# Expert 0 in one tile per batch, its first-batch tile computed between attention and experts

## The chip, the cores and the metric

The kernel runs on one core of a Trainium2 chip. A core has TensorE for matrix products, VectorE and ScalarE for elementwise work, GpSimd for odd jobs and for transfers by a list of addresses, and SyncE, which issues most transfers. Each engine works through its own instruction list in order and waits on semaphores for the others. The metric is the device time of one execution in microseconds (us).

## The reference

Three layers follow each other, for 2 batches of 768 tokens and a width of 512. First an attention in 8 heads of 64, where a query sees only the keys of its own cluster. Then a mixture of 8 experts:

```python
for b in range(B):
    prev_e = -1
    for s in range(S):
        fresh_e = int(np.argmax(logits[b, s]))
        if s == 0 or local_gate[b, s] < 0.5: e = fresh_e
        else: e = prev_e if prev_e >= 0 else fresh_e
        prev_e = e
        ...
        h = np.maximum(x[b, s] @ w1[e], 0.0)
        out[b, s] = p[e] * (h @ w2[e])
```

So each token goes to one expert, and which one depends on the tokens before it in its batch. `w1[e]` is 512 x 1024 and `w2[e]` 1024 x 512. Last comes a gated convolution over the tokens with two 512 x 512 products.

## The kernel before

**Precision.** Products of the experts are made in a fast format (fp32r) from split operands: a value is a high part (cast on ScalarE) plus a low part (the remainder, subtracted on VectorE). A product is three matmuls: high x high, low x high, high x low.

**Attention** runs over 96 items (a head, 128 queries) in 16 groups of 6, in one loop over `i`. Each item has scores (`do_S`), a row maximum on VectorE, an exponential on ScalarE, six transposes and their copies (`do_T`); products with the values follow one group later. Small pieces of other work are put at fixed values of `i`. The first batch is items 0 to 47 and its tokens are routed at items 54 to 69; the third quarter of the tokens is routed within the last group, the last quarter after it.

**Routing a quarter** (`route_steps`, r1 to r5) turns 384 tokens' logits into slot numbers: three small transposes on TensorE (r2p), a scan along the tokens on VectorE (r3), transposes back (r3p), a one-hot and counting matmuls (r4, r4p), slot numbers (r5). Then GpSimd scatters the 384 rows in three transfers (line 612) to `xslots` in DRAM, a list of slots per expert. Experts in `HALVED` have a list for each batch. A row has its 512 values, its gate value and its token number.

**Between attention and experts.** When the last routing matmuls are issued, TensorE computes on constants (`keep_warm` and the loops at lines 851 to 858) until the rows of expert 0 have been scattered and read back (`load_x(0)`, line 1002).

**Experts** are taken in 8 places `k`; four have a fixed expert (`AT`), the four others are ordered by their counts, which SyncE reads as registers (`turn`, line 1124). `CAPS[k]` is the number of slots that a place computes; what exceeds it goes through an overflow loop, which did not run in this execution. For each place `load_x` fetches rows, `do_x` transposes them (four transposes per tile of 128) and splits them, `do_mm1` makes the first layer (2 halves x 4 blocks x 3 terms x 4 depths = 96 matmuls over all columns, into hidden units high and low), and `do_mm2` the second (per tile of 128 rows, 24 matmuls of 512 columns), scaled and scattered by token number to `x2d`.

**Weights** of a place are four pieces of 1 MB, two of the first layer and two of the second. `worder` is the order in which pieces are used and `j` the index in it. `w_dma(j)` loads a piece into one of three staging buffers, `w_split(j, half)` splits half a piece: one ScalarE cast (line 342), one VectorE subtraction (line 343). Split pieces live in a ring of four. A list `work` holds splits and loads to come, and `tick()` takes one of them after each quarter of a first layer and each half tile of a second, besides steps of `overflow_steps` and of the conversion of the final weights.

**Memory.** Pools are stacked. When attention's SBUF pools close, staging buffers, ring and experts' tiles take their place, and their first writers wait for the last users of what lies below.

## Time and profile before

| what | us |
|---|---|
| median of 3 runs (lowest, highest) | 554.32 (554.28, 554.47) |
| the profiled execution's own time | 553.66 |
| span of its trace, first to last instruction | 551.6 |
| TensorE busy, VectorE busy, ScalarE busy | 530.4, 390.3, 333.9 |
| 108.22 MB moved, mean 196 GB/s | |

Times of the trace count from the first instruction. The time of an execution has 2.1 us around its span; the profiled one is 0.66 us under the median. A busy TensorE is not a useful one: constant matmuls count as busy, and matmuls overlap, so the pitch is read from the distance of starts and not from the length of one.

### The profile page before, as it was taken

What the parts mean: (1) busy time and instruction counts of PE and PEld (TensorE: products, weight loads), DVE (VectorE), ACT (ScalarE), POOL (GpSimd) and SP (SyncE); (2) the same over time, 40 slices, a digit from 0 to 9 for tenths busy, and PEclk for the clock granted to TensorE, in tenths of its full rate; (3) what the DMA queues carried; (4) which work ended last, traced back from release to release, by engine and by line L of the source; (5) the groups of instructions that cost most, each with busy time, mean ns of one, the idle gap of its engine ahead of it and who ended that gap; (6) DMA issues with size and microseconds to landing.
All of it is one profiled execution on the core that took longest, in us unless ns stands there. A gap on an engine that the chain in (4) does not pass through costs nothing. (4 is left out here: it accounts for less than half of the span.)

```text
span 551.6 us, 9244 instructions
## 1 busy us (share of the span) xinstructions
PE 530.4 (96%) x3393; PEld 425.4 (77%) x3394; DVE 390.3 (71%) x686; ACT 333.9 (61%) x612; POOL 108.0 (20%) x109
## 2 busy tenths in 40 slices
PE   7898999999999999998789999999999989999996
PEld 3766767776777767767589898878989788899885
DVE  5685767675787776636557988949896893499960
ACT  3696778676777777764145555637465564385642
POOL 4111010020212040111200234162435324100000
PEclk9899999999999999999899999999999999999999
DMA  5776797888784857221658767676876777640023
GB/s 144 218 165 201 166 302 170 265 211 252 215 252 144 212 164 159 106 76 55 219 213 297 229 231 272 213 289 220 293 276 243 243 241 262 211 192 0 20 95 114
DMA packets 35672, 108.22 MB, mean 196 GB/s; under 512 B 5096, under 2 KB 5608, under 8 KB 31016
## 3 DMA queue, kind: packets, MB, share of 16 engines
q1 hardware_dynamic: 31751, 98.61, 58.0%
q0 software_dynamic: 2912, 8.41, 4.0%
q10 hardware_dynamic: 960, 0.58, 0.4%
q8 instruction: 27, 0.44, 0.3%
q14 instruction: 22, 0.17, 0.1%
HBM read 58.83 MB, written 29.39 MB: 160 GB/s over the span
## 5 line engine op out<-in xcount | busy, mean ns | idle before, releaser
L652 DVE TENSOR_REDUCE mx<-s 128x1 f32<-128x768 f32 x96 | 91.5, 954 | 59.4 <-PE s L645 53.1
L681 ACT COPY pt<-tp 128x384 f32<-128x384 f32 x148 | 65.8, 484 | 53.7 <-PE tp L676 53.7
L661 ACT ACTIVATE pexp<-s,mx 128x768 f32<-128x768 f32 x96 | 87.2, 909 | 6.1 <-DVE mx L652 5.0
L343 DVE TENSOR_TENSOR wlo<-wraw,whi 128x1024 fp32r<-128x1024 f32 x62 | 86.9, 1417 | 4.9 <-ACT whi L342 4.6
L676 PE MATMUL tp<-ident,pexp 128*128 128x128 f32 x576 | 81.2, 277 | 0.3 <-DVE pt L679 0.2
L676 PEld LDWEIGHTS tp<-ident,pexp 128*128 128x128 f32 x576 | 68.2, 142 | 7.6 <-ACT pt L681 3.4
L342 ACT CAST whi<-wraw 128x1024 fp32r<-128x1024 f32 x64 | 65.0, 1047 | 8.5 <-DMA wraw<-in_wq_dram 8.5
L688 PE MATMUL pv<-pt,vt 128*64 128x384 f32 x360 | 67.8, 498 | 0.2 <-ACT ut L697 0.2
L641 PE MATMUL s<-st 128*128 128x384 f32 x188 | 57.4, 386 | 1.6 <-ACT pexp L661 1.5
L1082 PE MATMUL yp<-whi,hhi 128*128 128x512 f32 (+4 forms) x136 | 53.7, 395 | 0.8 <-PEq L1147 0.8
L1083 PE MATMUL yp<-wlo,hhi 128*128 128x512 f32 (+4 forms) x136 | 53.7, 395 | 0.1
L1084 PE MATMUL yp<-whi,hlo 128*128 128x512 f32 (+4 forms) x136 | 53.5, 393 | 0.0
L645 PE MATMUL s<-st 80*128 80x384 f32 x188 | 48.9, 341 | 1.3 <-DMA st<-ohr 1.3
L1061 ACT ACTIVATE hhi<-hps 128x512 fp32r<-128x512 f32 (+4 forms) x36 | 19.4, 538 | 45.2 <-PE hps L1057 42.9
L641 PEld LDWEIGHTS s<-st 128*128 128x128 f32 x188 | 28.6, 191 | 18.5 <-ACT pt L681 7.4
L1057 PE MATMUL hps<-xhi,whi 128*128 128x256 f32 (+4 forms) x256 | 41.6, 284 | 0.7 <-ACT xhi L1031 0.7
L1057 PE MATMUL hps<-xhi,wlo 128*128 128x256 f32 (+4 forms) x256 | 41.0, 281 | 0.7 <-DVE wlo L343 0.7
L1057 PE MATMUL hps<-xlo,whi 128*128 128x256 f32 (+4 forms) x256 | 41.1, 281 | 0.1
L688 PEld LDWEIGHTS pv<-pt,vt 128*64 128x64 f32 x360 | 21.9, 136 | 24.1 <-issue 23.7
L1062 DVE SCALAR_TENSOR_TENSOR hlo<-hps,hhi 128x512 fp32r<-128x512 f32 (+4 forms) x36 | 21.6, 608 | 23.4 <-ACT hhi L1061 20.8
L361 POOL TENSOR_TENSOR xx<-xkq,xx 128x768 fp32r<-128x768 f32 x8 | 14.5, 1817 | 117.8 <-ACT xx L355 117.8
L1057 PEld LDWEIGHTS hps<-xhi,whi 128*128 128x128 f32 x256 | 35.2, 189 | 1.7 <-ACT xhi L1031 1.1
(263 smaller groups left out, 928.9 us busy)
## 6 DMA issues: line engine op xcount, KB each, us to landing
wraw<-in_wq_dram SPq DMA_DIRECT2D x30, 1024.0 KB, 6.1
st<-xx SPq DMA_DIRECT2D x48, 384.0 KB, 4.0
xslots<-padrow SPq DMA_DIRECT2D x14, 771.0 KB, 11.9
xkq<-in_kq_dram SPq DMA_DIRECT2D x15, 384.0 KB, 4.3
wspace<-in_wd_dram SPq DMA_DIRECT2D x8, 512.0 KB
xall<-xnat SPq DMA_DIRECT2D x4, 771.0 KB
vt<-in_v_dram SPq DMA_DIRECT2D x8, 384.0 KB, 3.3
out_dram<-os SPq DMA_DIRECT2D x11, 256.0 KB, 2.0
```

The costliest lines, as they stand in the source:

```text
L342: nc.scalar.copy(hi[:, c], t[:, c])
L343: (lo_eng or nc.vector).tensor_tensor(lo[:, c], t[:, c], hi[:, c].bitcast(F32), op=ALU.subtract)
L641: nc.tensor.matmul(ps[:, n, :384], st[:, 1, q0:q0 + 128], st[:, 0, 384 * n:384 * n + 384], start=True, stop=False)
L652: nc.vector.tensor_reduce(mx, ps[:, :, :384], axis=AX.XY, op=ALU.max, negate=True)
L661: nc.scalar.activation(pt, ps[:, :, :384], AF.Exp, bias=mx[:, 0:1], accum_out=Zt[i // 6][:, t, h:h + 1])
L676: nc.tensor.transpose(tp[:, k, :], p[:, 128 * kt:128 * kt + 128], ident)
L681: nc.scalar.copy(dst, tp)
L688: nc.tensor.matmul(PVs[u][64 * h:64 * h + 64, :], Vt[g][:, kt, h, :], PT[u, h][:, kt, :], start=(kt == 0), stop=(kt == NQT - 1), skip_grou ...
L1057: nc.tensor.matmul(hp, a[:, d, fs], c[:, d, :w], start=(n + d == 0), stop=(n + d == 5))
L1082: nc.tensor.matmul(yp[:r], hhi[:, fa, ts], whv[:, f, :], start=(q == 0 and f == 0), stop=False)
L1083: nc.tensor.matmul(yp[:r], hhi[:, fa, ts], wlv[:, f, :], start=False, stop=False)
L1084: nc.tensor.matmul(yp[:r], hlo[:, fa, ts], whv[:, f, :], start=False, stop=(q == 1 and f == 3))
```

## The change

Expert 0 becomes an expert with a list for each batch (`HALVED`), and its place computes 128 slots, those of the second batch. The rows of its first-batch list are loaded at item 84 of attention (`early_load`), and transposed and split at item 89 (`early_rows`). The matmuls on constants go; in their place stand the 96 first-layer matmuls of this tile (`early_products`), put between the routing steps of the last quarter as 17, 11, 5 and the rest, into two PSUM banks `eh`. All four weight pieces of expert 0 now come first in `worder`. Pieces 2 and 3 are loaded by SyncE before the last quarter is routed, 4 and 5 behind the splits of 1 and 2, all ahead of `load_x(0)`; pieces 3 and 4 were loaded by GpSimd before, after expert 1's rows had come. VectorE subtracts pieces 1, 2 and 3 and makes the early tile's low parts behind the slot numbers, and the copies for `turn` come after these. The second layer of the early tile opens the experts' part, with `do_x(0)` before its last two blocks. Then come first and second layer of the second-batch tile, and expert 1. The constants of attention move to a pool that closes with it, and two input pools move to the right end of SBUF, where they stay until the early products are done.

```diff
...
-CAPS = (256, 256, 300, 240, 224, 184, 256, 256)
+CAPS = (128, 256, 300, 240, 224, 184, 256, 256)
...
-HALVED = (1, 2)
+HALVED = (0, 1, 2)
...
-    xin_p = apool("xin", 1)
-    xx_p = apool("xx", 1)
+    early_pools = ExitStack()
+    epool = lambda name: early_pools.enter_context(tc.tile_pool(name=name, bufs=1, side="right"))
+    xin_p = epool("xin")
+    xx_p = epool("xx")
+    acst = apool("acst")
...
-    cd = cst.tile([128, 4, 32], F32, name="cd")
-    cent_sb = cst.tile([128, 4, 64], F32, name="cent_sb")
+    cd = acst.tile([128, 4, 32], F32, name="cd")
+    cent_sb = acst.tile([128, 4, 64], F32, name="cent_sb")
...
-    worder = []
-    for k in range(E):
-        worder += [(k, 0), (k, 1)]
-        if k:
-            worder += [(k - 1, 2), (k - 1, 3)]
+    worder = [(0, 0), (0, 1), (0, 2), (0, 3), (1, 0), (1, 1)]
+    for k in range(2, E):
+        worder += [(k, 0), (k, 1), (k - 1, 2), (k - 1, 3)]
...
     def w_split(j, half, lo_eng=None):
         if worder[j][0] == E:
             return
+        w_high(j, half)
+        w_low(j, half, lo_eng)
+
+    def w_high(j, half):
         rp = ring(j)
...
+        nc.scalar.copy(hi[:, c], wraw[j][:, c])
+
+    def w_low(j, half, lo_eng=None):
+        hi, lo = W[worder[j]]
+        c = slice(1024 * half, 1024 * half + 1024)
         t = wraw[j]
-        nc.scalar.copy(hi[:, c], t[:, c])
         (lo_eng or nc.vector).tensor_tensor(lo[:, c], t[:, c], hi[:, c].bitcast(F32), op=ALU.subtract)
 
 
...
+    EA = {}
+
+    def early_load():
+        EA["xs"] = xin_p.tile([128, 2, S], F32, tag="x", name="exs")[:, 0, :XC]
+        nc.sync.dma_start(EA["xs"], xslots[0:128, :])
+
+    def early_rows():
+        xs = EA["xs"]
+        ids = EA["ids"] = small.tile([128, 1], I32, tag="eids", name="eids", bufs=1)
+        nc.vector.tensor_copy(ids, xs[:, 513:514])
+        pw = EA["pw"] = small.tile([128, 1], F32, tag="epw", name="epw", bufs=1)
+        nc.vector.tensor_copy(pw, xs[:, 512:513])
+        xp = ps_m.tile([128, 512], F32, tag="m", name="exp")
+        for d in range(4):
+            nc.tensor.transpose(xp[:, 128 * d:128 * d + 128], xs[:, 128 * d:128 * d + 128], ident)
+        xx = xx_p.tile([128, 4, S], F32R, tag="xx", name="exx")
+        hi, lo = EA["x"] = xx[:, 0, :512], xx[:, 1, :512]
+        nc.scalar.copy(hi, xp)
+        nc.vector.tensor_tensor(lo, xp, hi.bitcast(F32), op=ALU.subtract)
 
...
+        if i == 84:
+            early_load()
+        if i == 89:
+            early_rows()
     while route:
         route.pop(0)()
     last_PV(2)
+    eh = ps_s.tile([128, 2, 512], F32, tag="s", name="eh")
+    nc.vector.memset(eh[:, 1, :], 0.0)
...
+    w_dma(3)
     moe = ExitStack()
     mpool = lambda name, bufs=1, **k: moe.enter_context(tc.tile_pool(name=name, bufs=bufs, **k))
     ring1 = mpool("ring1", R - 1)
     rings[1] = ring1
-    for n, f in enumerate(route_steps(3)):
-        if n == 1:
-            last_rows()
-        f()
-
-    keep_warm(ps_t.tile([128, 512], F32, tag="t", name="spin3"), 10)
-    spin4 = ps_t.tile([128, 512], F32, tag="t", name="spin4")
-    for w in (128, 192, 224, 256):
-        for _ in range(8):
-            nc.tensor.matmul(spin4[:, :w], onesr[:, :128], onesr[:, :w], start=True, stop=True)
-    for w in (128, 192, 288):
-        for _ in range(6):
-            nc.tensor.matmul(spin4[:, :w], onesr[:, :128], onesr[:, w:2 * w] if w < 256 else onesr[:, :w], start=True, stop=True)
-
+    h_p = mpool("hp", 1)
+    WX = (max(CAPS[0::2]), max(CAPS[1::2]))
+    ehhi, ehlo = [h_p.tile([128, 8, WX[1]], F32R, tag=f"h{t}1", name=f"eh{t}") for t in ("hi", "lo")]
+
+    def early_products():
+        xhi, xlo = [t.rearrange("p (d c) -> p d c", d=4) for t in EA["x"]]
+        for q in range(2):
+            whv, wlv = [t.rearrange("p (d f) -> p d f", d=4) for t in W[0, q]]
+            terms = ((whv, xhi), (whv, xlo)), ((wlv, xhi),)
+            for part in (terms if q else (terms[0] + terms[1],)):
+                for f in range(4):
+                    for a, c in part:
+                        for d in range(4):
+                            yield nc.tensor.matmul(
+                                eh[:, q, 128 * f:128 * f + 128], a[:, d, 128 * f:128 * f + 128], c[:, d, :],
+                                start=(q == 0 and a is whv and c is xhi and d == 0), stop=(a is wlv and d == 3),
+                                skip_group_check=True,
+                            )
+
+    ep = early_products()
+
+    def early(n):
+        for _ in range(n):
+            next(ep, None)
+
+    def early_relu(q, c):
+        hp = eh[:, q, 256 * c:256 * c + 256].rearrange("p (f n) -> p f n", f=2)
+        nc.scalar.activation(ehhi[:, 4 * q + 2 * c:4 * q + 2 * c + 2, :128], hp, AF.Relu)
+
+    def early_rest(q, c):
+        fs = slice(4 * q + 2 * c, 4 * q + 2 * c + 2)
+        hp = eh[:, q, 256 * c:256 * c + 256].rearrange("p (f n) -> p f n", f=2)
+        nc.vector.scalar_tensor_tensor(
+            ehlo[:, fs, :128], hp, 0.0, ehhi[:, fs, :128].bitcast(F32), op0=ALU.max, op1=ALU.subtract
+        )
+
+    r1, r2p, r2d, r3, r3p, r4, r4p, r4d, r5 = route_steps(3)
+    r1()
+    w_high(1, 0)
+    w_high(1, 1)
+    last_rows()
+    early(17)
+    r2p()
+    r2d()
+    r3()
+    early(11)
+    r3p()
+    r4()
+    early(5)
+    r4p()
+    r4d()
+    r5()
+    for c in range(2):
+        w_low(1, c)
+    early(96)
+    w_dma(4)
+    for c in range(2):
+        w_split(2, c)
+    for c in range(2):
+        early_relu(0, c)
+        early_rest(0, c)
+    w_dma(5)
+    for c in range(2):
+        w_split(3, c)
+        early_relu(1, c)
+        early_rest(1, c)
 
...
+    YP = {}
     aps.close()
 
 
-    xs_p = mpool("xs", 1)
+    early_pools.close()
+    xs_p = mpool("xs", 1, side="right")
+    y_p = mpool("yp", 3, side="right")
     xt_p = mpool("xt", 1)
-    h_p = mpool("hp", 1)
-    y_p = mpool("yp", 3)
     mps = ExitStack()
-    qpool = lambda name, bufs=1: mps.enter_context(tc.tile_pool(name=name, bufs=bufs, space=PSUM))
+    qpool = lambda name, bufs=1: mps.enter_context(
+        tc.tile_pool(name=name, bufs=bufs, space=PSUM, reuse_waits="tile")
+    )
     ps_x = qpool("ps_x", 1)
     ps_h = qpool("ps_h", 4)
     ps_y = qpool("ps_y", 2)
...
+        if k == 0:
+            nc.sync.dma_start(XS[k][:, 0, :], xslots[E * SLOT:E * SLOT + 128, :])
+            return
...
-        for t in range(n) if k == 0 else ():
-            nc.sync.dma_start(XS[k][:r, t, :], src[:, t, :])
-        if k:
-            nc.sync.dma_start(XS[k][:r, :n, :], src)
+        nc.sync.dma_start(XS[k][:r, :n, :], src)
 
...
     load_x(1)
     for n, k in enumerate(free):
         turn[k] = nc.sync.value_load(ordi[0:1, n:n + 1], min_val=NF, max_val=E - 1)
-    nc.gpsimd.tensor_copy(gate[:TR[1], 2:3], XS[1][:TR[1], 1, 513:514])
-    w_dma(3, nc.gpsimd)
-    w_split(1, 0)
-    w_split(1, 1)
-    w_next(1, nc.gpsimd)
-    for j in range(2, R):
-        work.append(lambda j=j: w_split(j, 0))
-        work.append(lambda j=j: (w_split(j, 1), w_next(j)))
-    do_x(0)
-    work.insert(2, lambda: keep_rows(3))
+    w_dma(6)
+    ey = ps_y.tile([128, 512], F32, tag="y", name="ey")
+    for q in range(2):
+        whv, wlv = mm2_weights(0, q)
+        for f in range(4):
+            fa = 4 * q + f
+            if fa == 6:
+                do_x(0)
+            nc.tensor.matmul(ey, ehhi[:, fa, :128], whv[:, f, :], start=(fa == 0), stop=False)
+            nc.tensor.matmul(ey, ehhi[:, fa, :128], wlv[:, f, :], start=False, stop=False)
+            nc.tensor.matmul(ey, ehlo[:, fa, :128], whv[:, f, :], start=False, stop=(fa == 7))
+    y = y_p.tile([128, 512], F32, tag="y", name="ysb")
+    nc.scalar.activation(y, ey, AF.Copy, scale=EA["pw"])
+    scatter(x2d, EA["ids"], y, 2 * S, "rows of different tokens")
+    work += [lambda: None, lambda: None, lambda: keep_rows(3)]
     late += overflow_steps()
     do_mm1(0)
     XS["ready"] = True
-    for k in range(1, E - 1):
+    do_mm2(0)
+    do_mm1(1)
+    for k in range(2, E - 1):
         do_mm1(k)
         do_mm2(k - 1)
     do_mm1(E - 1)
```

## Rows read from the trace of the kernel before

**Rows 1.** By stretch: PE, PEld, DVE, ACT, POOL busy; granted clock, DMA share, GB/s.

```profile
160.00:200.00 40.00, 40.00 (x276) 28.58 (x275) 31.05 (x82) 28.72 (x64) 8.96 (x8) 1.00 0.72 218
...
280.00:300.00 20.00, 19.91 (x170) 19.80 (x170) 12.72 (x30) 9.82 (x14) 1.15 (x2) 1.00 0.70 251
```

**Rows 2.** Timeline of TensorE in the gap: start us, us, engine, line, tiles.

```profile
259.95 1.01 PE L753 MATMUL po<-wgl_sb,ut 128*128 128x146 f32 x6
...
262.92 0.49 PE L529 MATMUL rps<-ident,rr 128*1 128x128 f32 x3 [1.96 <-DVE rr L520]
...
264.68 0.34 PE L541 MATMUL rps<-ident,sc 1*128 1x1 f32 x3 [1.27 <-DVE sc L533]
...
269.33 3.98 PE L855 MATMUL spin<-onesr 128*128 128x128 f32 x32
...
273.15 2.29 PE L858 MATMUL spin<-onesr 128*128 128x128 f32 x18
...
276.36 1.31 PE L1026 MATMUL xp<-ident,xs 128*128 128x128 f32 x8 [0.92 <-DMA xs<-xslots]
...
278.38 1.00 PE L1057 MATMUL hps<-xhi,whi 128*128 128x256 f32 x4 [0.72 <-ACT xhi L1031]
...
284.81 1.04 PE L1026 MATMUL xp<-ident,xs 128*128 128x128 f32 x8
...
285.60 0.73 PE L1057 MATMUL hps<-xhi,whi 128*128 128x256 f32 x4
...
291.38 0.64 PE L1057 MATMUL hps<-xhi,whi 128*128 128x256 f32 x4
```

**Rows 3.** Timeline of ScalarE and VectorE: splits, slot numbers, evictions of 300 columns.

```profile
262.77 1.99 ACT L342 CAST whi<-wraw 128x1024 fp32r<-128x1024 f32 x2
...
266.60 0.16 DVE L596 TENSOR_TENSOR idx<-sl,ov 128x3 int32<-128x3 f32 x1
...
268.50 2.37 DVE L343 TENSOR_TENSOR wlo<-wraw,whi 128x1024 fp32r<-128x1024 f32 x2
...
317.86 0.42 ACT L1061 ACTIVATE hhi<-hps 128x300 fp32r<-128x300 f32 x1 [0.97 <-PE hps L1057]
...
319.06 0.46 DVE L1062 SCALAR_TENSOR_TENSOR hlo<-hps,hhi 128x300 fp32r<-128x300 f32 x1
```

**Rows 4.** Timeline of transfers issued by SyncE and GpSimd in the gap.

```profile
259.09 0.48 SPq L326 DMA_DIRECT2D wraw<-in_wq_dram  x1
...
269.61 0.98 POOL L612 DMA_INDIRECT xslots<-xnat,idx  x1 [0.30 <-issue]
...
273.53 0.80 SPq L1002 DMA_DIRECT2D xs<-xslots  x2
```

**Rows 5.** Timeline of TensorE, two starts of the second layer.

```profile
304.87 0.39 PE L1082 MATMUL yp<-whi,hhi 128*128 128x512 f32 x1
...
311.81 0.40 PE L1082 MATMUL yp<-whi,hhi 128*128 128x512 f32 x1
```

**Rows 6.** Busy time by stretch, as in rows 1, in the gap and after.

```profile
264.00:269.00 5.00, 4.02 (x20) 1.86 (x21) 3.98 (x22) 0.77 (x1) 1.66 (x2) 0.68 0.77 294
...
282.00:287.00 5.00, 5.00 (x46) 5.00 (x45) 3.16 (x9) 3.54 (x6) 0.00 (x0) 1.00 0.97 406
```

**Rows 7.** Scatters, median us to landing: from 264 us, and from 255 us.

```profile
xslots<-xnat,idx POOLq DMA_INDIRECT x3, 3.6
...
xslots<-xnat,idx POOLq DMA_INDIRECT x6, 5.9
```

**Rows 8.** Timeline of TensorE, scores that open four pairs of attention items.

```profile
216.56 0.62 PE L641 MATMUL s<-st 128*128 128x384 f32 x2
...
221.79 0.61 PE L641 MATMUL s<-st 128*128 128x384 f32 x2
...
226.25 0.62 PE L641 MATMUL s<-st 128*128 128x384 f32 x2
...
230.72 0.62 PE L641 MATMUL s<-st 128*128 128x384 f32 x2
```

More of the change, by code (lines that the diff above doesn't have):

```diff
@@ L124, in routed_attention_moe_kernel, with const_iota @@
     )
-    def const_iota(name, shape, pattern, base, mult=0):
-        t = cst.tile(shape, F32, name=name)
+    def const_iota(name, shape, pattern, base, mult=0, at=cst):
+        t = at.tile(shape, F32, name=name)
         nc.gpsimd.iota(t, pattern=pattern, base=base, channel_multiplier=mult, allow_small_or_imprecise_dtypes=True)
         return t
-    wts = const_iota("wts", [128, 24, NC_], [[0, 24], [-1, NC_]], NC_)
+    wts = const_iota("wts", [128, 24, NC_], [[0, 24], [-1, NC_]], NC_, at=acst)
     ewt = const_iota("ewt", [128, 2, 3, V], [[0, 2], [0, 3], [-1, V]], E)
@@ L157, in routed_attention_moe_kernel @@
         nc.gpsimd.memset(capk[:, :, n], float(CAPS[k]))
-    wgl_sb = cst.tile([128, 4, 146], F32, name="wgl_sb")
+    wgl_sb = acst.tile([128, 4, 146], F32, name="wgl_sb")
     nc.scalar.dma_start(wgl_sb[:, :, 128:146], wgl)
@@ L181, in fill_slots @@
         yield nc.sync.dma_start(xslots[rows - n:rows, :], padrow[:n])
-    csq = cst.tile([128, 4, 64], F32, name="csq")
+    csq = acst.tile([128, 4, 64], F32, name="csq")
     cs = cst.tile([128, 6, 4], F32, name="cs")
@@ L982, in routed_attention_moe_kernel @@
     TR = [c // n for c, n in zip(CAPS, NT)]
-    WX = (max(CAPS[0::2]), max(CAPS[1::2]))
     XS = {}
@@ L1072, in do_mm1 @@
         HT[k] = (hhi, hlo)
-    YP = {}
     def mm2_part(k, t, q, whv, wlv):
```

## The prediction

> **What bounds the kernel now.** I read the stage table first. Right after the gap TensorE is busy 19.91 of 20 us [rows 1]: the expert phase runs at TensorE's own pace, so a matmul taken out of it is worth its pitch, as long as weights and rows keep up. Next the timeline of the gap between attention and experts [rows 2]. The last attention matmuls end at 260.96. Then TensorE does three short routing pieces and fills the rest with matmuls on constants (32 from 269.33, 18 from 273.15). Expert 0's rows arrive for transposing at 276.36, and its first product starts at 278.38. So from 261 to 278.4 TensorE is in use but earns nothing. What ends this gap is a chain that TensorE is no part of: the slot numbers are ready on VectorE at 266.76 [rows 3], GpSimd issues the last of three scatters at 269.61, and SyncE, which waits for them to land, issues the load of expert 0's rows at 273.53 [rows 4].
>
> **Prices.** Three kinds of TensorE work count.
> Second-layer matmuls (512 columns): from 304.87 to 311.81 lie 30 of them [rows 5], 0.2313 us each, so a tile of 24 costs 5.55 us.
> First-layer matmuls, 256 columns: from 285.60 to 291.38 lie 48 (half of expert 0) [rows 2], 0.120 us each.
> First-layer matmuls, 128 columns: the nearest rows are the 32 constant matmuls, eight each of 128, 192, 224 and 256 columns, 3.82 us from 269.33 to 273.15 [rows 2], 0.119 us each. The mean over four widths equals the 256-column pitch, so width is not what they pay for, and I take 0.119 for 128 columns. (If 256 columns had cost twice what 128 do, this mean could not have come out so.)
> Hence halving the columns of expert 0's first layer saves nothing: 96 matmuls before, 96 early plus 96 later now. The change can only win by what moves ahead of the rows' arrival.
>
> **What the move is worth.** Before, expert 0's first layer ends at 291.38; taking off 96 x 0.120 and the 0.79 us of eight transposes (284.81 to 285.60) [rows 2], it is as if it had started at 279.0 and run without a stall. From there expert 0 still owes 96 + 48 matmuls. After, it owes 96 + 24 from its start T: the other second-layer tile lies ahead of T. So the net is (T - 279.0) - 5.55 us, plus what attention pays.
>
> **When T comes.** The early products: 17 between the last logits and the first routing transposes (2.0 us from 260.96, so to 263.0, where the transposes begin at 262.92 now), 11 under the scan (1.3 us from 263.4, where the next step begins at 264.68), 5 before the count [rows 2]. They fill holes nearly to the tenth; I charge the routing chain 0.2 us. The other 63 follow from about 266.0 and take 7.5 us, to 273.5. They need weight 1's low half, which VectorE now makes right after the slot numbers (two pieces, 2.37 us [rows 3], so 269.2); it is used only by the last 16, after 271.6: no stall.
> The second layer of the early tile needs weights 2 and 3 split. VectorE: weight 2 from 269.2 to 271.6; then two remainders of 128x256 at most 0.46 each, the 128x300 row [rows 3]; weight 3 and two more remainders until about 275.7. ScalarE: four casts of 1.0 each [rows 3] and four evictions of at most 0.42. The matmuls from 273.5 reach their seventh of eight blocks after 18, at 277.7, after these are done. The copies that give SyncE its expert numbers now come last on VectorE, near 277; what waits for them on SyncE is the load of weight 6, needed only for expert 2.
> At 277.7 the program puts the four transposes of expert 0's second-batch rows (0.40), then the last six matmuls (1.39). With rows there, T = 279.5. Without, all of TensorE's queue waits behind these transposes.
>
> **When the rows come.** This is the term I am least sure of. Today the load goes out at 273.53 with nothing ahead of it, and the transposes start 2.83 us later. Now SyncE has issued weights 2, 3 (after the last logits, since weight 2's buffer covers the logits' weights), 4 (when weight 1 is split, 269.3) and 5 (when weight 2 is split, about 272) ahead of it: 1 MB each, where before it had issued weight 2 only [rows 4]. Lower bound: no delay, transposes at 276.4. Upper bound: everything in the order of issue. From 259.5 there are 771 KB of kept rows, two sets of scatters of 771 KB each and four weights, 6.6 MB; at the 406 GB/s of the densest stretch that is 16.2 us, at the 294 GB/s of the gap itself 22.3 [rows 6], so 275.7 to 281.8, then 0.8 for the load: 276.4 to 282.6. Contention is visible in the trace: the scatters of this gap land 3.6 us after issue, with little beside them, and with those of the quarter before, which ran beside 1.8 MB of SyncE's transfers, the median of six is 5.9 [rows 7].
> The Trainium skill (DMA: Bandwidth & Descriptors, Queues, rings and completion order) says each of the 16 engines takes turns between queues by packet and serves one queue in ring order; by it the load could not pass weight 5, and T would lie in the upper half of this range (a net of -2.7 to +0.4 us). The two medians agree with the turns; no run here shows a load stuck behind a weight.
> I take 279.0, near the middle: two weights are in front, but much of them moves while the scatters land. Then T = 279.0 + 0.40 + 1.39 = 280.8.
>
> **Attention pays.** Item 89 gets four transposes, one cast and three VectorE instructions. Bounds: the pair of items that carries a weight cast (1.0 [rows 3]) took 4.47 us (226.25 to 230.72) against 4.46 for its neighbour (221.79 to 226.25), so nothing; the pair with six more matmuls and their VectorE work took 5.23 (216.56 to 221.79), so 0.77 [rows 8]. The new piece resembles the second: 0.6. The cleared half bank is written while VectorE waits for the last logits: 0; were that cover gone, under 1 us (128x300 takes 0.46 [rows 3]). The load of the early rows is issued at item 84, five items ahead: 0. One more fill transfer and one more column in the routing's small tiles: 0, the transfers of attention lie beside its matmuls.
>
> **Later.** Expert 0 loses two of the slots in which weights are split and the final weights converted one step at a time. The order of the splits keeps its distance to their use (below), and some three conversion steps slide behind the half tiles that follow; their result is read only in the last stage: 0, with the half tile's 5.55 us as cover. The PSUM banks are now released tile by tile instead of all together; the banks of the early tile are read out by 275.7, before the transposes want them: 0.
>
> **Sum.** 280.8 - 279.0 - 5.55 + 0.6 = -3.2 us (the routing chain's 0.2 is inside the rows' arrival). The profiled execution took 553.66 us (span 551.6), so 550.5; the median of the runs is 0.66 above it, 554.32, so I forecast 551.2. Bounds of this case: T from 279.5 (with attention at 0) to 282.8, an arrival at 281.0 (with attention at 0.77): 549.3 to 553.3.
>
> **Rivals.**
> *Rows there in time* (by 277.7): T = 279.5, net -4.5, 549.9. For it: the scatters alone need 3.6 us, and weight 4's megabyte can be through by then. Against: weight 5 goes out about 272.
> *Rows too late*: SyncE's queue keeps the load behind weights 4 and 5 and the scatters wait for packets too. For an arrival from 281.0 to the upper bound of 282.6 the net is -1.0 to +0.4, so 553.3 to 554.8; at 282.2 nothing is gained. For it, the two medians; against, 406 GB/s is reached where two weights run side by side.
> *The clock* (the other side): TensorE's granted clock fell to half, the 1.2 GHz level, inside this gap, mean 0.68 over 264 to 269 [rows 6], after it had been mostly idle from 261. Now it is kept busy there, but by 128-column products, and again by 96 of them in expert 0's main part. If such a stream is granted 1.2 GHz, a product costs up to 0.24: 27 of them in the main part lose the whole gain, and all 96 cost 11.4 us, net +8.2: 562.5. Against it: attention, whose transposes are 128 columns wide, holds full clock [rows 1], though wider products lie between them. The Trainium skill (TensorE: Matmul & The Clock Gate, HAM oscillation) warns that thin products parted by transfer waits fall back to half rate again and again; by it the wait for rows before the main part would cost a stretch like the one seen, some 3.2 us at half, 1.6 us, net -1.6. No run here shows it for such a wait: the one that ends at 278.4 was followed by full clock, 1.00 from 280 to 300 [rows 1].
> *Expert 1's weights late*: its first layer now follows one tile, not two; the second piece of weight 5 is split under that layer's first quarter (2.9 us), and cast plus subtraction need 2.2 behind an eviction. If VectorE lags by one weight (2.4 us), net -0.8: 553.5. Before, expert 1's second half was fed the same way.
> That the first expert overflows its 128 rows per batch is excluded: routing the reference's inputs gives it 54 and 88 tokens.
>
> **Chances.** Forecast 0.60, rows in time 0.16, rows too late 0.10, clock 0.08, weights late 0.06. One measurement of this kernel tells about 0.2% (1.1 us) from no change, so faster means under 553.2. Faster: 0.60 + 0.16 + 0.02 of weights late = 0.78; same: 0.08 of rows too late and 0.04 of weights late = 0.12; slower: clock 0.08 and 0.02 of rows too late = 0.10. The range leaves out the clock, most of rows too late and little below: 548.9 to 554.0.
>
> **What would show it.** Early products at 0.119 us pitch, the 63 ending near 273.5; second-layer matmuls from there; transposes of expert 0's rows at about 279, waiting for their load and nothing else; first layer of expert 0 at 0.12 pitch with full clock; then one tile's 24 and expert 1, with TensorE as busy as now. The forecast is wrong if the load lands after 282, if the clock row shows 0.5 for long behind 266, if weight 2 or 3 is not split by 276, or if attention ends over 1 us later.

## The result and the profile after

The changed kernel takes 557.37 us (median of 21 runs, 554.51 to 562.89), the kernel before 554.09 beside it; the ratio is 1.0055 (1.0041 to 1.0069). It is slower by 0.55%. Forecast was 551.2, in a range of 548.9 to 554.0. The profiled execution took 557.47 us (span 555.4 against 551.6), so it stands for the median. Medians here are over all executions; the ratios leave out those over 1.5% above the fastest of their kernel (562.89 here, 562.84 in c1, 596.27 in c2).

The stage windows of the changed kernel (columns as in [rows 1]) go through the gap and two stretches behind it:

```profile
262.00:264.00 2.00, 1.88 (x18) 1.71 (x17) 1.74 (x8) 1.90 (x4) 0.73 (x1) 1.00 0.90 228
264.00:266.00 2.00, 1.63 (x21) 1.48 (x21) 1.50 (x9) 0.33 (x1) 0.00 (x0) 1.00 1.02 311
266.00:268.00 2.00, 2.00 (x13) 2.00 (x12) 1.79 (x7) 0.11 (x1) 0.98 (x1) 0.58 0.97 400
268.00:270.00 2.00, 2.00 (x11) 2.00 (x11) 2.00 (x3) 1.88 (x2) 1.70 (x2) 0.50 0.99 404
...
276.00:278.00 2.00, 2.00 (x12) 2.00 (x11) 0.00 (x0) 0.00 (x0) 0.00 (x0) 0.50 1.00 420
...
280.00:282.00 2.00, 2.00 (x6) 1.56 (x5) 1.32 (x2) 2.00 (x4) 0.00 (x0) 0.50 0.22 32
282.00:284.00 2.00, 2.00 (x7) 1.57 (x6) 2.00 (x4) 0.67 (x2) 0.00 (x0) 0.65 0.94 356
284.00:286.00 2.00, 2.00 (x12) 1.68 (x12) 1.52 (x11) 0.00 (x0) 0.00 (x0) 1.00 0.02 7
...
288.00:300.00 12.00, 12.00 (x105) 11.79 (x104) 3.70 (x17) 3.40 (x8) 0.98 (x1) 1.00 0.66 216
317.00:321.00 4.00, 4.00 (x23) 4.00 (x22) 2.66 (x6) 0.33 (x1) 0.00 (x0) 0.57 0.55 183
```

Read the clock beside PE's busy time. TensorE is busy for 1.88 and 1.63 of 2.00 us in the two windows ahead of the fall, and from 266.3 to 283.4, where it has half the clock, the 1.2 GHz level, it is idle only once, for 0.53 us. Expert 0's later products, just as thin, run from 287.25 to 298.77 at full clock. Another half stretch lies at 317 to 321.

The timeline of the same execution shows what those windows were spent on:

```profile
259.56 1.01 PE L762 MATMUL po<-wgl_sb,ut 128*128 128x146 f32 x6
...
260.61 11.26 SPq L327 DMA_DIRECT2D wraw<-in_wq_dram  x4
...
266.88 4.63 DVE L352 TENSOR_TENSOR wlo<-wraw,whi 128x1024 fp32r<-128x1024 f32 x4
...
267.01 1.94 POOL L621 DMA_INDIRECT xslots<-xnat,idx  x1 [4.28 <-DVE idx L605]
...
268.34 7.03 PE L895 MATMUL eh<-exx,whi 128*128 128x128 f32 x32
...
269.26 1.97 POOL L621 DMA_INDIRECT xslots<-xnat,idx  x1 [0.30 <-ACT whi L346]
...
271.53 0.98 POOL L621 DMA_INDIRECT xslots<-xnat,idx  x1 [0.30 <-issue]
...
275.16 3.62 PE L895 MATMUL eh<-exx,wlo 128*128 128x128 f32 x16
...
278.88 0.38 ACT L909 ACTIVATE ehhi<-eh 128x256 fp32r<-128x256 f32 x1 [9.00 <-PE eh L895]
...
279.31 0.79 PE L1220 MATMUL ey<-whi,ehhi 128*128 128x512 f32 x1 [0.53 <-ACT ehhi L909]
...
280.42 0.33 SPq L1082 DMA_DIRECT2D xs<-xslots  x1
...
285.42 0.60 PE L1115 MATMUL xp<-ident,xs 128*128 128x128 f32 x4
...
287.25 0.56 PE L1146 MATMUL hps<-xhi,whi 128*128 128x128 f32 x4
...
304.39 0.64 PE L1146 MATMUL hps<-xhi,whi 128*128 128x256 f32 x4
...
315.90 0.73 PE L1115 MATMUL xp<-ident,xs 100*128 100x100 f32 x6 [2.29 <-DVE xlo L1122]
```

**The gap.** 32 early products take from 268.34 to 275.16, 0.213 us each, where the constants they replace took 0.119 [rows 2]; the last early product starts behind 278 and not before 273.5. The first eviction starts only when all of them are done (9.00 us idle on ScalarE), the second layer behind it at 279.31, its first ten products at half clock. Expert 0's own first layer starts at T = 287.25, 6.45 us behind the forecast 280.8. Its transposes at 285.42 wait for nothing.

**The rows.** The load of expert 0's rows goes out at 280.42, 6.9 us later than before [rows 4]. SyncE's wait in front of it, in the list of SyncE's waits:

```profile
SPq L1082 <- DMA xslots<-xnat,idx: 8.5, 1, 8.5
```

From the last scatter's issue to that load lie 8.9 us (271.53 to 280.42), where there were 3.9 [rows 4]. This did not show in T only because the clock made the second layer later still: with the 2.83 us of before from load to transposes, the rows were there by about 283.2.

**Behind the gap.** Expert 1 starts at 304.39. Before, its place was 291.38 + 48 x 0.2313 = 302.5 [rows 2, 5], so 1.9 us are lost there. By the prediction's own formula: (287.25 - 279.0) - 5.55 = 2.7, less 0.8 because expert 0's products took 0.112 and not 0.120. Expert 2's second transposes then wait 2.29 us for VectorE; before, this wait was

```profile
301.43 0.73 PE L1026 MATMUL xp<-ident,xs 100*128 100x100 f32 x6 [0.82 <-DVE xlo L1033]
```

and the half clock behind it costs 1.7 (half of 3.4). That makes 1.9 + 1.5 + 1.7 = 5.1. At the last second-layer product (477.27 against 473.91) 3.4 are left. Of the other 1.7, 1.2 came back in the last expert's first layer, which takes 12.15 us and not 13.32: before, it waits 0.71 us there for a weight's low half. From the last second-layer product to the first of the final stage it is 3.35 us instead of 2.67, with a wait of 0.69 for x2nat in it, which makes 4.0; the spans differ by 3.8, so 0.2 comes back in the final stage.

### The profile page after: what moved, and what is told of

Same layout as the page of the kernel before. It is cut to its first block, busy times and chain, and to the rows that moved or that the text cites. A ratio compares the mean times of both kernels' runs of the same rounds, so it can differ in the third digit from the quotient of the medians.

```text
span 555.4 us, 9319 instructions
## 1 busy us (share of the span) xinstructions
PE 536.4 (97%) x3429; PEld 434.2 (78%) x3430; DVE 388.4 (70%) x694; ACT 333.9 (60%) x617; POOL 106.9 (19%) x108
## 5 line engine op out<-in xcount | busy, mean ns | idle before, releaser
L352 DVE TENSOR_TENSOR wlo<-wraw,whi 128x1024 fp32r<-128x1024 f32 x62 | 84.9, 1385 | 6.2 <-ACT whi L346 6.0
L1169 PE MATMUL yp<-whi,hhi 128*128 128x512 f32 (+4 forms) x128 | 50.5, 395 | 0.7 <-PEq L1241 0.7
L1170 PE MATMUL yp<-wlo,hhi 128*128 128x512 f32 (+4 forms) x128 | 50.4, 394 | 0.1
L1171 PE MATMUL yp<-whi,hlo 128*128 128x512 f32 (+4 forms) x128 | 50.3, 393 | 0.0
L1150 ACT ACTIVATE hhi<-hps 128x512 fp32r<-128x512 f32 (+5 forms) x36 | 18.5, 513 | 44.2 <-PE hps L1146 44.2
L1146 PE MATMUL hps<-xhi,whi 128*128 128x256 f32 (+5 forms) x256 | 41.5, 285 | 0.0
L1146 PE MATMUL hps<-xhi,wlo 128*128 128x256 f32 (+5 forms) x256 | 41.3, 284 | 0.0
L1151 DVE SCALAR_TENSOR_TENSOR hlo<-hps,hhi 128x512 fp32r<-128x512 f32 (+5 forms) x36 | 20.5, 579 | 29.5 <-ACT hhi L1150 29.2
L1146 PE MATMUL hps<-xlo,whi 128*128 128x256 f32 (+5 forms) x256 | 40.9, 282 | 0.0
L370 POOL TENSOR_TENSOR xx<-xkq,xx 128x768 fp32r<-128x768 f32 x8 | 14.6, 1821 | 116.4 <-ACT xx L364 116.4
L654 PEld LDWEIGHTS s<-st 80*128 80x128 f32 x188 | 34.1, 189 | 3.1 <-issue 1.7
```

What stands on the lines that cost most here:

```text
L352: (lo_eng or nc.vector).tensor_tensor(lo[:, c], t[:, c], hi[:, c].bitcast(F32), op=ALU.subtract)
L654: nc.tensor.matmul(ps[:, n, :384], st[0:80, 2, q0:q0 + 128], st[0:80, 3, 384 * n:384 * n + 384], start=False, stop=True)
L1146: nc.tensor.matmul(hp, a[:, d, fs], c[:, d, :w], start=(n + d == 0), stop=(n + d == 5))
L1169: nc.tensor.matmul(yp[:r], hhi[:, fa, ts], whv[:, f, :], start=(q == 0 and f == 0), stop=False)
L1170: nc.tensor.matmul(yp[:r], hhi[:, fa, ts], wlv[:, f, :], start=False, stop=False)
```

## The experiments

Each ratio is to the kernel before on the same chip.

**a1: early products late, the clock held by constants.** The products that filled the routing's holes are replaced by constant matmuls of 512 columns; all 96 follow the count.

```
-    early(17)
+    keep_warm(spin3, 10)
...
-    early(11)
+    keep_warm(spin3, 6)
...
-    early(5)
+    keep_warm(spin3, 2)
```

> Changed kernel, but the three holes between the last routing steps are filled with constant products of 512 columns (10, 6 and 2) instead of 17, 11 and 5 early products; all 96 early products follow the last routing step. Clock theory: TensorE's granted clock stays at or near 1.0 behind 266 us, the early products run at 0.11 to 0.12 us each and end near 277 instead of 278.9 although 33 more of them stand there, the second layer behind them takes 0.23 and not 0.43 each, and the time falls by 2 to 4 us against the changed kernel, to 553 to 555.5. Late-rows theory: the load of expert 0's rows still goes out near 280.4, its transposes can't start before 283, and the time falls by 2 us at most, 555 or more.

**a2: the rows' load ahead of weights 4 and 5.** Both `w_dma` move behind the two `load_x`.

```
     early(96)
-    w_dma(4)
...
-    w_dma(5)
...
     load_x(1)
+    w_dma(4)
+    w_dma(5)
```

> Changed kernel, but SyncE issues weights 4 and 5 behind the loads of expert 0's and expert 1's rows instead of ahead of them. Late-rows theory: the scatters land 4 to 5 us after their issue instead of 8, the load goes out between 275 and 278, and the time falls by 3 us or more, to 554 or less. Clock theory: TensorE is busy at half clock until 287 whatever the rows do, so the load goes out earlier and the time stays within 1 us of the changed kernel's 557.4.

**a3: both edits.**

> Both edits together: wide constant products in the holes, and weights 4 and 5 behind the row loads. If clock and late rows each hold back the changed kernel, as two limits one behind the other, this one is faster than either edit alone by 1 us or more: first layer of expert 0 from 281 to 283, 551.5 to 553.5. If the clock alone counts, it equals the first edit within 0.5; if late rows alone count, it equals the second.

Measured: a1 556.12 (ratio 1.0032, 1.0007 to 1.0056), a2 557.42 (1.0052, 1.0032 to 1.0071), a3 554.56 (1.0002, 0.9985 to 1.0019). Against the changed kernel's median the edits give 1.3 us and nothing alone, 2.8 together. The 1.3 is not clear of noise (the intervals of a1 and of the change overlap) and lies with the late-rows forecast of a1, not with its clock forecast. With the rows early the constants are worth 2.9 us (a3 against a2, clear of noise). So the two causes lie side by side, and the later one counts. a2 came out as its clock theory said; a1 and a3 stay above the times forecast for them (553 to 555.5, and 551.5 to 553.5).

In a1's and a3's profiles the granted clock is 1.00 over the whole of 262 to 284. In a1 the load then goes out at 279.91 and the transposes come at 282.77; in a3 at 276.75 and 282.13. a1's profile is of one of its slower executions (558.98): its expert 0 starts 2.6 us sooner than in the changed kernel (284.64), and the time is lost again behind the gap, where expert 2's transposes wait 2.90 us.

The clock is 1.00 in a2's profile too; that execution, 554.56, was its fastest, and the other five had a lower mean clock, 0.971 to 0.975 against 0.980. Its timeline shows the other two causes by themselves:

```profile
273.62 0.98 POOL L621 DMA_INDIRECT xslots<-xnat,idx  x1 [0.30 <-issue]
...
276.90 0.33 SPq L1080 DMA_DIRECT2D xs<-xslots  x1
...
299.46 0.64 PE L1144 MATMUL hps<-xhi,whi 128*128 128x256 f32 x4
...
310.97 0.73 PE L1113 MATMUL xp<-ident,xs 100*128 100x100 f32 x6 [2.29 <-DVE xlo L1120]
```

The load goes out 3.3 us after the last scatter's issue and not 8.9. Expert 1 starts at 299.46, 3.0 sooner than in the kernel before (302.5), and yet the span is 0.9 longer (552.5 against 551.6): 3.9 us are lost behind the gap.

What holds a3 back is a third thing, its first eviction:

```profile
276.78 0.38 ACT L909 ACTIVATE ehhi<-eh 128x256 fp32r<-128x256 f32 x1 [7.27 <-PE eh L895]
```

**b1: the kernel before, with weights 3 and 4 ahead of the rows.** No early tile; only the loads stand as in the change.

```
     w_dma(2)
+    w_dma(3)
...
+    w_split(1, 0)
+    w_split(1, 1)
+    w_next(1)
     load_x(0)
```

> The kernel before with nothing of the change but the order of transfers: SyncE issues weight 3 right behind weight 2 and weight 4 behind the split of weight 1, both ahead of the load of expert 0's rows (weight 5 stays where it was). Late-rows theory: the scatters compete with 2 MB, the load goes out 1.5 to 5 us later than 273.5, TensorE idles as long, and the time rises by as much, to 555.5 to 559. Clock theory: nothing of it matters, the transfers fit beside the scatters, 554 to 554.6.

Measured 557.39 (1.0057, 1.0039 to 1.0075), 2.9 us. The profiled execution was the fastest, 554.83; its timeline:

```profile
269.28 0.98 POOL L612 DMA_INDIRECT xslots<-xnat,idx  x1 [0.30 <-issue]
...
274.84 0.80 SPq L1003 DMA_DIRECT2D xs<-xslots  x2
...
277.74 1.29 PE L1027 MATMUL xp<-ident,xs 128*128 128x128 f32 x8 [1.58 <-DMA xs<-xslots]
```

There the load goes out 5.6 us after the last scatter's issue instead of 3.9, and the rows come 1.4 us later than before [rows 2], so the order of the loads alone delays them. The rest of the 2.9 lies in executions without a profile and is not accounted for.

**c1: the conversion later.** The steps that convert the final weights start one half of expert 0 later, and three beats in eight take a second step, not one in four, so that none is left at the end (counted in the program's lists: before 0, after the change 2).

```
     do_mm1(0)
-    XS["ready"] = True
     do_mm2(0)
+    XS["ready"] = True
...
-            if conv and beats[0] % 4 == 3:
+            if conv and beats[0] % 8 in (2, 5, 7):
```

> Changed kernel with one thing in the experts' part put back: the conversion of the final weights starts with expert 1's first layer, as before the change, and not with expert 0's second; its extra steps come 3 in 8 ticks instead of 1 in 4, so that none is left for the end. VectorE theory (after the gap the changed kernel loses time where expert 2's rows are split behind conversion steps on VectorE, to the clock that falls after that wait, and to conversion steps left over at the end): the 2.3 us wait of expert 2's transposes for the low part falls to 1 us or less, no half-clock stretch follows near 317, the last stage no longer waits 0.7 us or more for its reload, and the time falls by 2.5 to 4 us, to 553.4 to 555. Gap theory (clock and late rows in the gap explain all of it): no change, 556.5 to 558.

Measured 556.73 (1.0042, 1.001 to 1.0074), the time of the gap theory. What the VectorE theory said of the trace came true: the wait at expert 2 falls from 2.29 to 0.59, no half clock follows it, and the last stage doesn't wait for its reload. The median says little here, for the executions fall into two groups: five took 553.5 to 554.4 us, seven 556.1 to 562.8, and the mean clock does not part them (0.977 to 0.988 against 0.974 to 0.984). The profiled execution (560.65) is of the second group and shows the gap in its other form. Timeline and windows:

```profile
271.52 1.95 PE L895 MATMUL eh<-exx,wlo 128*128 128x128 f32 x16
...
283.14 1.09 PE L1115 MATMUL xp<-ident,xs 128*128 128x128 f32 x4 [4.53 <-DMA xs<-xslots]
...
286.58 0.95 PE L1146 MATMUL hps<-xhi,whi 128*128 128x128 f32 x4
```

```profile
282.00:283.00 1.00, 0.00 (x0) 0.00 (x0) 0.00 (x0) 0.00 (x0) 0.00 (x0) 0.69 1.02 350
283.00:298.00 15.00, 14.86 (x64) 14.32 (x65) 2.14 (x15) 2.10 (x5) 0.98 (x1) 0.50 0.56 193
298.00:299.00 1.00, 1.00 (x8) 1.00 (x6) 0.03 (x1) 0.32 (x1) 0.00 (x0) 0.50 0.00 0
299.00:300.00 1.00, 1.00 (x9) 1.00 (x8) 0.21 (x1) 0.76 (x2) 0.00 (x0) 0.77 0.00 0
```

With full clock the early products are done by 273.5, as forecast. Then TensorE waits 4.53 us for the rows, the clock falls within that wait, at 282.4, and stays at half for 17.1 us, although TensorE is not idle behind the wait. The load went out at 280.31, as in the changed kernel; from load to transposes it took 2.83 us, exactly as before [rows 2, 4]. What was late is the scatters, not the load.

**c2: all three edits of a1, a2 and c1.**

> Three edits on the changed kernel: constant products in the holes, weights 4 and 5 behind the row loads, and the conversion as in the run with that edit alone. If the three losses are separate they add up: 551 to 552.5, faster than the kernel before by 0.3 to 0.6%. If the wait of expert 2's transposes is only a consequence of the gap, this equals the kernel with the two gap edits, 554 to 555.

Measured 553.07 (0.9976, 0.9962 to 0.999): 1.5 us below a3 (1.4 by the ratios), between its two forecasts. In the profiles the stretch from expert 1's start to the first product of the final stage takes 174.0 us in c2 and 176.4 in a3.

**c3: c2, and the early sums in two tiles**, so that the first half is evicted while the second is computed.

```
-    eh = ps_s.tile([128, 2, 512], F32, tag="s", name="eh")
+    eh = [ps_t.tile([128, 512], F32, tag="t", name=f"eh{q}") for q in range(2)]
...
-    early(96)
+    early(48)
...
         early_rest(0, c)
+    early(96)
```

> The three edits, and the early products in two PSUM tiles, with the eviction of the first half issued ahead of the second half's products. Theory that the eviction chain sets expert 0's start: with one tile the first eviction waits for all 96 products (276.8 in the run with both gap edits); now the first half is evicted near 272 to 273, weight 3 is split by 278, expert 0's transposes come at 279 to 280.5 instead of 282.1, and the time falls by another 1 to 2 us, 549.5 to 551.5. Rival: rows or scatters set it, then the transposes stay at 280.5 or later and the time falls by less than 0.7.

Measured 550.98 (0.9942, 0.9928 to 0.9957), 2.1 us below c2 (1.9 by the ratios). The first eviction now waits for half of the products:

```profile
272.51 0.39 ACT L909 ACTIVATE ehhi<-eh 128x256 fp32r<-128x256 f32 x1 [2.21 <-PE eh L895]
```

The transposes come at 281.79, not at 279 to 280.5, and c2's came at 281.78; but attention ended 1.4 us later in this execution (the slot numbers at 267.80, c2's at 266.36). From the slot numbers to expert 0's first product it is 15.8 us, in c2 17.3.

**d1: wide early products, no constants.** a2 and c1; beside them high and low rows stand side by side, so that one product of 256 columns makes two terms: 64 early products instead of 96, the halves added at eviction.

```
+   o = eh[2 * q + f // 2][:, 256 * (f % 2):256 * (f % 2) + (256 if a is whv else 128)]
+   c = x2[:, d].rearrange("p h c -> p (h c)")[:, :256 if a is whv else 128]
...
+   nc.scalar.copy(es, hp[:, :, 1, :])
+   nc.vector.tensor_tensor(es, es, hp[:, :, 0, :], op=ALU.add)
```

> No constant products in the gap; weights and conversion as in the three edits. The early products are 64 instead of 96: high and low rows of the tile side by side as 256 columns for the high weights (32 matmuls), 128 for the low ones (32); the two halves are added at the eviction (one more copy on ScalarE, one more addition on VectorE each). Clock theory: a stream of wider products in the holes keeps TensorE's clock at 1.0 behind 266 in most executions, and the products end near 270 to 271 at 0.12 each; the rows then set the start, 281 or so, and the time is 549.5 to 552. If width does not matter to the clock, it falls at 266 as in the changed kernel, the 31 products behind the routing take 0.22 each, and the time is 1 us or more above that.

Measured 550.63 (0.9939, 0.9924 to 0.9953), as c3 without its constants. Its clock stays at 1.00 through the routing's holes. After two waits of 0.53 and 0.69 us for weight 1's low half it falls at 272.8, within a third wait, 1.27 us for the first eviction, but only for 6.8 us:

```profile
270.00:272.00 2.00, 1.30 (x12) 1.26 (x12) 2.00 (x3) 0.52 (x2) 1.70 (x2) 1.00 0.87 351
273.00:279.00 6.00, 5.21 (x12) 4.14 (x13) 3.53 (x8) 3.77 (x8) 0.96 (x1) 0.50 0.44 145
280.00:290.00 10.00, 10.00 (x80) 9.47 (x80) 4.16 (x26) 3.39 (x8) 0.98 (x1) 1.00 0.87 314
```

**e4: SyncE's expert numbers first.** In the changed kernel the small VectorE instructions that order the experts move ahead of weight 1's subtractions, so the scatters are issued before these run.

```
     r5()
+    tot = lt_p.tile([128, V], F32, tag="tot", name="tot")
...
     for c in range(2):
         w_low(1, c)
```

> Changed kernel with one edit: the nine short VectorE instructions for the expert numbers stand right behind the slot numbers again, ahead of the subtraction of weight 1, as before the change. Theory that VectorE's long subtractions hold up GpSimd's scatters (each takes 1.94 to 1.97 us instead of 0.98 where a subtraction was already running): the first two scatters take 0.98 again, the last is issued about 2 us sooner, near 269.7, and the load of expert 0's rows goes out 1 to 2 us sooner, 278.4 to 279.5. Rival (the scatters are slow because the transfers are busy): they still take 1.94. The time moves by less than 1 us in either case, since the clock sets the start.

Measured 557.57 (1.0038, 1.0008 to 1.0067), no gain at the median. The timeline of its scatters and subtractions:

```profile
267.34 0.98 POOL L621 DMA_INDIRECT xslots<-xnat,idx  x1 [4.29 <-DVE key L938]
...
268.62 0.98 POOL L621 DMA_INDIRECT xslots<-xnat,idx  x1 [0.30 <-issue]
...
268.72 4.63 DVE L352 TENSOR_TENSOR wlo<-wraw,whi 128x1024 fp32r<-128x1024 f32 x4
...
269.90 2.04 POOL L621 DMA_INDIRECT xslots<-xnat,idx  x1 [0.30 <-issue]
```

The load goes out at 278.79, 1.6 earlier than in the changed kernel, but the clock is at half again (0.51 over 267 to 284) and the first eviction at 278.63. Its 12 runs split by clock: three with a mean granted clock of 0.994 to 1.0 took 551.3, 551.6 and 554.5 us, nine with 0.967 to 0.982 took 556.2 to 559.4. So the same program is faster or slower than the kernel before (554.15 beside it), and here its time goes with the clock.

**e1, e2: the same order in c3 and in d1.**

> The kernel with the three edits and two PSUM tiles, and the short VectorE instructions ahead of the subtractions. If the scatters now set expert 0's start: its transposes come 1 to 2 us sooner than in that kernel (281.8), and the time falls by 0.5 to 1.5 us to 549.5 to 550.5. If the eviction and split chain sets it, the 1.6 us by which VectorE's subtractions move back costs as much as the scatters win: 551 within 0.5.

> The kernel with wide early products, and the short VectorE instructions ahead of the subtractions. The wide products of the second half wait for weight 1's low part already (two waits of 0.5 to 0.7 us), so the subtractions moving back by 1.6 us cost up to 1.6 there, while the load of the rows goes out 1 to 2 us sooner than 276.6: 550 to 551.5, that is no gain, if the chain on VectorE sets the start; 549 to 550 if the rows do.

Measured: e1 550.65 (0.9939, 0.9919 to 0.9959), no different from c3; e2 552.02 (0.9964, 0.995 to 0.9978), rather worse than d1 and above both of its forecasts. In e2 the subtractions end later, the wide products need them early, and they wait 2.05 us where d1's waited 0.53.

**e3: e2, and expert 0's remaining tile in wide products too**, 64 instead of 96.

```
+                    if k == 0:
+                        for a in (whv, wlv):
+                            for d in range(4):
+                                c = x2[0][:, d].rearrange("p h c -> p (h c)") if a is whv else xhi[:, d]
```

> The same, and expert 0's second tile made in 64 wide products too instead of 96 of 128 columns (with one more copy and addition at each of four evictions). If a 128-column product costs TensorE as much as one of 256, 32 fewer are worth 32 x 0.12 = 3.8 us where TensorE sets the pace: 546 to 548. If the evictions or the weights of expert 1 set the pace there, less than 1.5 of it shows.

Measured 548.88 (0.9904, 0.9882 to 0.9926), 3.1 us below e2 and so 0.9 above the range for a TensorE that sets the pace. Expert 0's tile in e3, first product to first of the second layer, and below it in c3, on the timelines:

```profile
283.07 0.86 PE L1157 MATMUL hps<-x2w,whi 128*128 128x256 f32 x4
...
291.45 0.45 PE L1198 MATMUL yp<-whi,hhi 128*128 128x512 f32 x1
```

```profile
283.62 0.56 PE L1146 MATMUL hps<-xhi,whi 128*128 128x128 f32 x4
...
295.14 0.45 PE L1169 MATMUL yp<-whi,hhi 128*128 128x512 f32 x1
```

8.38 us for 64 products against 11.52 for 96, with eight transposes in each: a product left out is worth 0.098 us, though half of those that stay are twice as wide.

## Why the prediction was wrong

**The clock (rival, given 0.08).** This is the step that failed first: the 63 early products behind the routing were charged 0.119 us each, and 32 of them took 0.213. The prediction asked whether 128-column products, in expert 0's main part, would be granted full clock, and answered by attention, where they are mixed with wider ones [rows 1]. In the main part it was right: 1.00 over 288 to 300, 0.112 us each. It didn't ask what the thin products do in the gap, where the clock fell before too, after idle pieces [rows 6], and where the removed constants of 512 columns had stood. The clock fell at 266.3 and stayed down for 17.1 us. Price: the 63 products ended 5.3 us late and the second layer's first ten took 0.2 more each. It does not fall in every execution. Of four profiles with thin products in the holes it fell behind the routing in two (after, e4); a2 and c1 went through the same products at 1.00. With constants in the holes it was 1.00 through the gap in all five (a1, a3, c2, c3, e1), with products of 256 and 128 columns there (d1) up to 272.8. What decides between the two cases is not shown, nor is a1's gain alone clear of noise.

The Trainium skill (TensorE: Matmul & The Clock Gate, HAM oscillation) tells of thin products parted by waits for transfers, which start at half rate again after each wait. The prediction weighed such a wait for rows at 3.2 us at half; c1 shows one, but with 17.1 us at half behind it, and in the changed kernel the longest wait of TensorE in the 6 us ahead of the fall was 0.37 us.

**"When the rows come": 279.0, upper bound 282.6.** The load went out at 280.4, which with the 2.83 us of [rows 2, 4] is 283.2, past the bound. The bytes of the bound were sized well: 6.4 MB had moved from 259.5 to 279.5, between its 275.7 and 281.8. But it allows 0.8 us for the load behind them, where the lower bound has 2.83. And the choice of 279.0, because much of the weights moves while the scatters land, fails on two things. The scatters take 8.9 us from the last issue to the load beside weights 3 to 5, and not 3.9; that it is the order of the loads, a2 (3.3), a3 against a1 (5.1 against 8.0) and b1 (5.6 against 3.9) show. And the last issue came 1.9 us later: two of three issues took 1.94 and 1.97 us instead of 0.98, because they began while a subtraction of weight 1 or 2 was running, longer by about what was left of it; in e4 only the issue that began under one was long.

The Trainium skill (SBUF — State Buffer, SBUF: two separate sides) says that a VectorE instruction with two inputs in SBUF and a GpSimd instruction that reads SBUF lock each other out, the one that starts first for its whole length. These rows agree for GpSimd's side only: the subtraction that began 0.1 us behind an issue (e4, 268.72) took 1.23 us, the others 1.22. Weight 5 did not hold up the load itself: the transfers were at 32 GB/s over 280 to 282, when the load went out.

**The evictions "by 275.7".** They were costed by duration and their place on the engines, not by what they wait for. Both halves of the early sums lie in one tile, and the first eviction waited for the last product, in whatever state the clock was (9.00 us after, 7.27 in a3). Weight 3's casts stood behind them on ScalarE, at 280.03 and 281.24. Two tiles gave 2.1 us (c3 against c2), 1.4 of them in the profiles between the slot numbers and expert 0's first product. Of the four signs that the prediction named for being wrong, three came true: the clock's row, a weight not split by 276, and, by the 283.2 above, a load that lands after 282.

**"Later: 0".** The conversion is started by a flag between the two layers of expert 0, and with one tile there expert 1 and 2 come two slots sooner behind it. Its VectorE steps then met the splits of expert 2's rows, a wait of 2.29 for 0.82, and the clock fell behind it. c1 takes the wait away; c2 against a3 puts all of it, tail included, at 1.5 us by the medians and 2.4 by the profiles, and a2's profiled execution lost 3.9 us behind the gap. That the steps' result is read only in the last stage was true, and no reason for 0: they take VectorE's time when they run.

**What was right.** A second-layer tile out of the main part (5.55 us), the 0.12 us of a product of 128 columns as of 256 (0.112 at full clock), and the early products done by 273.5 when the clock is full (c1). With the four causes removed the kernel takes 551.0 (c3) or 550.6 (d1), where 551.2 was forecast; that the numbers meet is in part luck. In their profiles expert 0 starts 15.8 and 14.6 us behind the slot numbers, where the forecast has 14.2 (280.8 behind 266.6), and the thinner products gave back 0.8 that the sum didn't count. What attention pays can't be read from one profile: the last logits came at 259.56, 0.4 sooner than before [rows 2], but at 259.5 to 261.6, 260.3 in the mean, in the twelve profiles with the early tile against 259.95 and 259.50 in the two without it. So the 0.6 is neither confirmed nor refuted.

## What to carry to other kernels

Before you replace matmuls that only keep TensorE busy, look at what they did for the granted clock, and read it again with the useful products in their place: here products of 128 columns did not always keep it, those of 256 beside 128 kept it through the holes in every profile (d1, e2, e3). Cost a moved transfer by who else is in flight when it lands, and a moved VectorE instruction by what GpSimd issues beneath it; ask of each eviction which product of its whole tile comes last. Moving a stage by one tile shifts every list that advances by slots, so look for who shares VectorE with the next stage.

## What the runs showed of the hardware

A stream of 128-column products, with some transposes in it, ran at either clock for long: at full clock for 11.5 us (after, 287.25 to 298.77), at half for 12.5 us (after, 266.3 to 278.8) and 12.9 us (c1, 286.6 to 299.4). The three stretches at half in which it stood (after, c1, e4) lasted 17.1 us each; those in which 512-column products ran instead lasted 3.4 us (before) and 6.8 us (d1). What ends a long one is not settled: after the change 512-column products had run for 4 us, in c1 only transposes and thin products.

A scatter's issue on GpSimd takes 0.98 us, or 1.94 to 2.04 when it begins with 1.1 to 1.2 us of a VectorE subtraction of 128x1024 left to run; one that began 0.1 us ahead of it took 0.98 (e4, 268.62).

At full clock a product of 256 columns took 0.13 us in e3 and one of 128 took 0.10 (0.112 where there were only such), so two terms that share their weights are worth putting side by side: 32 products fewer gave 3.14 us in expert 0's tile.
